# Two gated-mix attention branches on one core: the output product's features put in the order "place by head", one tile of inverted denominators per block, and the output weights rearranged once in DRAM

## The chip, the core and the metric

The kernel runs on one core of a Trainium2 chip. The metric is the time of the slowest core (here the only one) in microseconds of one execution, taken on the device. The work is split among TensorE (PE, with its weight loads PEld), VectorE (DVE), ScalarE (ACT), GpSimd (POOL) and SyncE (SP), whose only work here is to issue every DMA of the kernel.

## What is computed

The same attention layer is computed twice on one input x (2048 tokens, 640 features), with the weights of a branch A and of a branch B, and the two results are mixed by a gate of each token. Each branch has 32 heads of 20 features and treats the tokens in 4 segments of 512:

```
q, k, v = x @ wq, x @ wk, x @ wv               # 32 heads of 20
g = sigmoid(beta)                              # one per head
M, z = 0, 0
for s in range(4):                             # segments of 512 tokens
    logits = qs @ ks.T * 20**-0.5 + mask       # causal within the segment
    a_dot = softmax(logits) @ vs
    a_mem = (phi(qs) @ M) / (phi(qs) @ z + 1e-6)
    o = g * a_mem + (1 - g) * a_dot
    M, z = M + phi(ks).T @ vs, z + sum(phi(ks))
branch = concat(o) @ wo
out = gate * branch_A + (1 - gate) * branch_B  # gate = sigmoid(x . gate_w)
```

Here phi(t) is t + 1 above zero and exp(t) below.

## The kernel before

The work is cut into 8 **blocks** t = 0..7: block t is segment t // 2 of branch t % 2. Within a block there are 8 **quads** of four heads (i = 8 t + u). Products are formed with activations and weights split into a high and a low part (hi, lo), as three terms. TensorE's array is used as two halves of 64 rows that run different instructions side by side (`ROWS`).

Per block, `job_qk` and `job_v` form q, k and v. The parts of q and k are written to DRAM (`hi_lo_out`, L724) and read back by quad with the features of one head on the partitions (`load_quads`, L1136). `s_unit` (L1178) forms the scores and VectorE takes each row's maximum straight out of the PSUM bank (L1165); the maximum is sent into the q tile by a small DMA (L1215). `t_unit` (L1268) forms the transposed scores, ScalarE exponentiates (L1260) and GpSimd clears what lies above the diagonal (L1261). `pv_unit` (L1288) multiplies by v with a column of ones, so row 20 of each head's 32 rows is the softmax denominator; the result is copied to SBUF (L1318). For blocks 0 to 6 `send_dot` writes it to the DRAM tile `dots[t]` (L1332): 32 heads of 32 rows, 512 tokens long. Block 7 goes another way (`fin_unit`), which the change leaves in the order by feature.

For blocks 0 to 6 the softmax numerators then have to be divided by their denominators, weighed with the gates and added to the memory's part. This stage, called the **mix** below, goes as follows. `spread` (L644, L646) lays the token gate out over 16 heads. `reciprocals(t, g, d)` works on half g of the heads: it fetches the 16 denominator rows as a 128 x 64 tile `dn` (L1374), multiplies and inverts them on VectorE (L1354, L1356), writes them to `recs` (L1359), and widens each row 20 times in DRAM into `wide[t]` (L1364, 640 KB read and written). `mix(t, k, y, r)` then fetches, for 128 of the 640 features, the numerators from `dots[t]` in 2 or 3 pieces (L1413: 120, 100, 16, 12, 8 or 4 rows, cut where a head straddles the edge) and the widened inverses from `wide[t]` (L1414), and multiplies the two on VectorE or GpSimd (L1410, L1411). With the memory's part, transposed on TensorE from the tile O (L1493) and added on VectorE (L1473), it is split into hi and lo (L1391 to L1394), and `job_o` multiplies it by the output weights wo (L1018). The first half of the heads can be mixed when the quads 0 to 3 of the block are done, the second when all 8 are.

The order of all instructions is written by a **planner** inside the kernel. It keeps a clock, a list of due times and a queue for each engine, and it emits an instruction when its model says that its inputs have arrived. `dma(us, emit, then, ...)` is what it assumes of a transfer: `us` of bandwidth and `lat` until it has landed. The table `RULES` holds, for each quad, eight numbers that shift its choices. On the chip every engine runs its list in the order written: what the planner believed too early is waited for, with everything behind it on that engine. The tiles `row0` to `row27` (`big`) are a pool of 128 x 512 buffers, shared by all stages. The framework gives SP's transfers eight semaphores in turn, and an issue waits for the transfer eight places before it to have landed.

The lines of `mix` that load:

```
for f, n, src in parts_of:
    dma(0.0055 * n, ... out=r32(y[f:f + n, :]), in_=src ...)          # L1413
dma(0.7, ... out=r32(r), in_=wide[t][P * k:P * k + P, :] ...)          # L1414
```

Of the kernel before, what the change touches and what calls it, by code (L numbers as in the profile page):

```python
# [18 lines left out]
P = 128  # L19
D = 640  # L20
# [22 lines left out]
def tile_gated_mix_infini_attn(  # L43
# [122 lines left out]
    def start_next(e):  # L166
# [11 lines left out]
        def end():  # L178
            busy[e] = False
            load[e] -= dur  # L180
            if then:
                at(clk[0] + DONE[e], then)
# [1584 lines left out]
```

## Time and profile before

| What | Value |
|---|---|
| Times of three runs | 1053.37, 1049.56, 1052.10 us; median 1052.1 us |
| The profiled execution's own time | 1050.84 us |
| Its span, first to last instruction | 1049.1 us |
| Mean granted TensorE clock | 0.989 |
| TensorE busy (weight loads) | 1014.1 us (858.9 us) |
| VectorE, ScalarE, GpSimd busy | 758.6, 661.2, 582.6 us |
| DMA engines' mean share, bytes moved | 77.5%, 249.5 MB |
| Issues of SP | 1133 |

The profile is one execution. A row of its groups reads: line, engine, operation, output<-input by the program's names, sizes, count, then busy time and mean of one instruction, then how long the engine sat idle just before such instructions and what ended that. `bank` is a PSUM bank, `row` a buffer of the pool, `wst` a tile of raw weights, `wh` and `wl` its two parts. A view of stretches gives, for each stretch of the span, the busy time and count of each engine, the granted clock, the DMA engines' mean busy share and the GB/s that they moved. The view of the DMA queue in order of time gives start, time and line of each run of issues on SP; the time is that of issuing, not of landing.

### The profile page before, as it was taken

To read this page: it belongs to the slowest core of one execution; us is meant where nothing else is said; L and a number is where in the kernel's file an instruction comes from. 1 tells how busy PE (TensorE), PEld (TensorE's weight loads), DVE (VectorE), ACT (ScalarE), POOL (GpSimd) and SP (SyncE) were. 2 spreads that over 40 slices of the span, in tenths; PEclk is the share of its full clock that TensorE was granted. 3 is DMA by queue.
4 is the path that set the end of the run, shared out by engine and by line. 5 is a ranking of instruction groups with operands and counts; after the bars stand their busy time and mean duration, and the time that the engine had idled before them with its cause. 6 is when DMAs were issued, how large, how long until landed. Compare 5 with 4: busy or idle time off the path is not lost.

```text
span 1049.1 us, 31149 instructions
## 1 busy us (share of the span) xinstructions
PE 1014.1 (97%) x11260; PEld 858.9 (82%) x11260; DVE 758.6 (72%) x2632; ACT 661.2 (63%) x1344; POOL 582.6 (56%) x1020
## 2 busy tenths in 40 slices
PE   9999998999999999989999999999999999999998
PEld 7888887788887898878889777887888977778876
DVE  4777786766796777866778776788667866776854
ACT  6377676577655566746756556575666665666472
POOL 4455565556454655755655655575565545647271
PEclk9999999999999999989999999999999999998999
DMA  7898978878787888867978778897779878868631
GB/s 258 281 314 242 304 229 260 245 252 260 198 270 216 262 270 247 282 185 236 288 202 268 207 253 264 246 285 206 244 241 272 259 236 259 265 187 258 166 119 55
DMA packets 138399, 251.53 MB, mean 240 GB/s; under 512 B 20085, under 2 KB 24213, under 8 KB 138245
## 3 DMA queue, kind: packets, MB, share of 16 engines
q1 hardware_dynamic: 138244, 249.54, 77.5%
q8 instruction: 89, 1.46, 0.6%
q14 instruction: 66, 0.53, 0.2%
HBM read 159.88 MB, written 97.96 MB: 246 GB/s over the span
## 4 chain that ended last, share of the span: by engine, by line
PE 70%; DMA 16%; DVE 4%; SPq 4%; ACT 2%; issue 2%; POOL 2%; DVEq 0%; ACTq 0%; POOLq 0%
PE bank L744 41%; PE bank L1288 11%; PE bank L1268 6%; PE bank L1178 6%; DMA row<-wide 4%; PE bank L934 2%; PE bank L854 2%; PE bank L894 2%; SPq L1413 2%; DVE bank L1165 2%; DMA wst<-in_b_wv_dram 1%; DMA qd<-row 1%; DMA qst<-qd 1%; DMA row<-dots 1%; DMA kst<-kd 1%
## 5 line engine op out<-in xcount | busy, mean ns | idle before, releaser
L1165 DVE CUSTOM_DVE_ANT_0 bank<-bank,tri 128x384 f32<-128x384 f32 (+3 forms) x1024 | 475.3, 520 | 155.2 <-PE bank L1178 119.1
L744 PE MATMUL bank<-row,wh 64*128 64x512 f32 x2308 | 503.8, 404 | 1.1 <-DVE row L701 1.1
L1260 ACT ACTIVATE p<-bank 128x512 f32<-128x512 f32 x582 | 319.9, 600 | 138.8 <-PE bank L1268 102.7
L1261 POOL TENSOR_SCALAR_AFFINE_SELECT p<-p 128x256 f32<-128x256 f32 (+1 forms) x582 | 217.8, 384 | 251.6 <-ACT p L1260 239.0
L744 PEld LDWEIGHTS bank<-row,wh 64*128 64x128 f32 x2308 | 318.4, 186 | 13.6 <-DVE row L701 1.3
L744 PE MATMUL bank<-row,wl 64*128 64x512 f32 x1154 | 304.7, 401 | 0.0
L536 POOL TENSOR_TENSOR wl<-wst,wh 128x640 fp32r<-128x640 f32 x115 | 180.1, 1570 | 66.2 <-ACT wh L534 64.1
L1268 PE MATMUL bank<-qst,kst 62*128 62x384 f32 (+3 forms) x1024 | 180.9, 323 | 17.8 <-DVE mx L1165 7.0
L1178 PE MATMUL bank<-kst,qst 60*128 60x384 f32 (+3 forms) x1024 | 181.3, 318 | 5.4 <-DVE mx L1165 3.3
L744 PE MATMUL bank<-wvh,row 64*128 64x320 f32 x1280 | 184.8, 316 | 0.7 <-DVE mx L1165 0.7
L744 PEld LDWEIGHTS bank<-row,wl 64*128 64x128 f32 x1154 | 178.3, 187 | 5.5
L1268 PEld LDWEIGHTS bank<-qst,kst 62*128 62x128 f32 x1024 | 132.6, 188 | 30.3 <-DVE mx L1165 10.2
L744 PEld LDWEIGHTS bank<-wvh,row 64*128 64x128 f32 x1280 | 153.3, 187 | 2.6 <-DVE mx L1165 0.9
L1178 PEld LDWEIGHTS bank<-kst,qst 60*128 60x128 f32 x1024 | 133.6, 187 | 15.3 <-DVE mx L1165 5.9
L1288 PE MATMUL bank<-p,vst 128*32 128x256 f32 (+3 forms) x1920 | 145.6, 427 | 0.2 <-DVE mx L1165 0.2
L1165 DVE DVE_READ_ACCUMULATOR2_ANT mx<- 128x1 f32 x1024 | 145.6, 142 | 0.0
L1288 PEld LDWEIGHTS bank<-p,vst 128*32 128x32 f32 x1920 | 58.6, 110 | 85.0 <-issue 62.1
L744 PE MATMUL bank<-wvl,row 64*128 64x320 f32 x640 | 105.3, 313 | 0.0
L534 ACT CAST wh<-wst 128x640 fp32r<-128x640 f32 x119 | 87.0, 742 | 28.1 <-PE bank L744 14.0
L744 PEld LDWEIGHTS bank<-wvl,row 64*128 64x128 f32 x640 | 84.3, 186 | 0.2
L511 POOL TENSOR_TENSOR wvl<-wst,wvh 128x640 fp32r<-128x640 f32 (+1 forms) x48 | 63.9, 1336 | 21.4 <-ACT wvh L508 20.4
L1318 ACT COPY row<-bank 128x512 f32<-128x512 f32 x55 | 32.5, 592 | 56.2 <-PE bank L1288 45.8
(117 smaller groups left out, 1175.7 us busy)
## 6 DMA issues: line engine op xcount, KB each, us to landing
qd<-row SPq DMA_DIRECT2D x120, 256.0 KB
kd<-row SPq DMA_DIRECT2D x120, 256.0 KB
qst<-qd SPq DMA_DIRECT2D x128, 240.0 KB
kst<-kd SPq DMA_DIRECT2D x128, 240.0 KB
dots<-row SPq DMA_DIRECT2D x56, 256.0 KB
wide<-recs SPq DMA_DIRECT2D x14, 640.0 KB
row<-wide SPq DMA_DIRECT2D x35, 256.0 KB
wst<-in_a_wq_dram SPq DMA_DIRECT2D x20, 320.0 KB
```

The costliest lines, as they stand in the source:

```text
L511: put("G", 0.77 * n, lambda: nc.gpsimd.tensor_tensor(out=wl[:, a:b, :], in0=w3, in1=r32(wh[:, a:b, :]), op=ALU.subtract), end, prio=4)
L534: put("A", 0.625, lambda: nc.scalar.copy(wh, w3), lambda: put(lo_eng, lo_cost, lambda: lo.tensor_tensor(out=wl, in0=w3, in1=r32(wh), op=AL ...
L536: lambda: lo.tensor_tensor(out=wl, in0=w3, in1=r32(wh), op=ALU.subtract), end, prio=3), prio=6)
L744: return nc.tensor.matmul(bank_of, lhsT=w[ROWS[half]], rhs=x_[ROWS[half]], start=start, stop=stop)
L854: return nc.tensor.matmul(pm[:, a - h0:c - h0, :].rearrange("p h e -> p (h e)"), lhsT=r32(pqTs[t, m][ROWS[half], P * n:P * (n + 1)]), rhs= ...
L1165: put("D", w / 960.0 + 0.105, lambda: nc.vector.tensor_tensor_reduce(out=sc[:, off:off + w], in0=sc[:, off:off + w], in1=tri[:, L - w:], s ...
L1178: lane_ops[half].append((mm(w), lambda pair=pair, qb=qb, off=off, w=w, r=r, sc=sc: nc.tensor.matmul(sc[:, off:off + w], lhsT=q[r, pair, P ...
L1260: put("A", 0.483, lambda: nc.scalar.activation(pt, sc, AF.Exp, scale=SCALE), lambda: (bank.give(sc), put("G", 0.15 + 0.105 * len(todo), la ...
L1261: "G", 0.15 + 0.105 * len(todo), lambda: nc.gpsimd.affine_select(out=blocks, in_=blocks, pattern=[[0, len(todo)], [1, P]], base=0, channel ...
L1268: lane_ops[half].append((mm(w), lambda pair=pair, kb=kb, off=off, w=w, r=r, sc=sc: nc.tensor.matmul(sc[:, off:off + w], lhsT=k[r, pair, P ...
L1288: nc.tensor.matmul(po[32 * j:32 * j + 32, P * kb:], lhsT=vst[t % 2][:, kb, h * E1:h * E1 + 32], rhs=pts[i, n, f][0][:, off:off + w], start ...
L1318: either(0.483, lambda: nc.scalar.copy(r32(oT), po), 0.605, lambda: nc.vector.tensor_copy(r32(oT), po), end, 2)
```

## The change

1. Features of the output product. The 640 features of blocks 0 to 6 are put in the order "place e within the head, then head h" (32 e + h), where they stood in the order 20 h + e. The memory's part is written to the tile O in that order (`by_head`, at L871), so a tile of 128 features holds 4 places of all 32 heads.
2. Loads of the mix. With that order the numerators of one tile are one DMA, 4 places by 32 heads (L1434 of the new kernel), in place of 2 or 3 pieces.
3. Inverted denominators. The 128 lanes of every one of the five feature tiles need the same 32 inverses, four times over. So one tile d of 128 x 512 is fetched (L1392, the denominators of all heads, 4 times), multiplied with the token gate, fetched straight from `rowg` to all partitions (L1394), and inverted in two halves of 256 columns. It serves all five multiplies. `spread`, `recs`, `wide`, the two halves of heads and their tiles go away; the mix of a block starts when all 8 quads are done.
4. Output weights. wo of both branches must have its rows in the new order. `mix_weights` does it once in DRAM, from due times 75 and 215 of the planner's clock: five DMAs to `wrow` (row-major), five to `wmix` (rows reordered, 4 places by 32 heads each). 35 loads of wo (blocks 0 to 6) then read 5 pieces of 128 columns per partition from `wmix`; the five of block 7 stay as they were.
5. The high part of q and k goes to its two places in DRAM with one DMA of 512 KB in place of two of 256 KB.
6. The planner: SP's next issue also waits until the eighth-last transfer is assumed to have landed; the assumed times of most transfers are raised (0.7 to 0.82 or 0.87, 0.84 to 1.05) and their latencies lowered (2.0 to 1.6); `RULES` is another table. With it the order of the instructions differs throughout the program.

SP issues 940 DMAs in place of 1133, counted in the two programs. TensorE has the same number of matmuls.

```diff
     RULES = {
-        0: "TSTSTSTSTS 1.010 1.98 0.35 8 0.0 1.6 1.92",
...
+        0: "TSTSTSTSTS 1.010 2.38 0.30 8 0.0 1.6 1",
...
-        if e == "S" and dma_free[0] > clk[0] + BACKLOG:
...
+        if e == "S":
+            begin_at = max(dma_free[0] - BACKLOG, lands[-LANES] if len(lands) >= LANES else 0.0)
...
+        if kind == "o":
+            src = [wmix[t % 2].rearrange("k p n -> p k n")[:, :, P * c:P * c + P] for c in range(KT)]
...
+    def mix_weights(b):
+        def rows(k):
+            if k == KT:
+                blocks(0)
+                return
+            dma(2.0, lambda: nc.sync.dma_start(
+                out=wrow[b][k].rearrange("p (m n) -> p m n", n=P),
+                in_=weights[b]["o"].rearrange("m p k n -> k p m n")[k]), prio=500)
+            at(clk[0] + 3.0, lambda: rows(k + 1) if k + 1 < KT else at(clk[0] + 6.0, lambda: blocks(0)))
+
+        def blocks(c):
+            heads = wrow[b].rearrange("k p n -> (k p) n").rearrange("(h e) n -> e h n", e=DH)
+            dma(2.0, lambda: nc.sync.dma_start(
+                out=wmix[b][c].rearrange("(e h) n -> e h n", h=H), in_=heads[4 * c:4 * c + 4]),
+                (lambda: mixed_there.add(b)) if c == KT - 1 else None, prio=500)
...
-                for c in places:
-                    dma(0.7, lambda c=c, part_=part_: nc.sync.dma_start(
-                        out=r32(dst[P * m:P * (m + 1), c, :]), in_=r32(part_)), one, prio=-1)
+                dma(0.7 * n, lambda n=n, places=places, part_=part_: nc.sync.dma_start(
+                    out=r32(dst[P * m:P * (m + 1), places, :]),
+                    in_=r32(part_)[:, None, :].to_broadcast([P, n, L])), sent, prio=-1)
...
+        rec_asked.add(t)
+        big.want((F32, F32), lambda d, g: reciprocals(t, d, g), prio=1)
         for k in range(KT):
...
+            big.want((F32,), lambda y, k=k: mix(t, k, y), prio=2)
+
+    def lanes_of(t):
+        return dots[t].rearrange("(h r) n -> r h n", r=32)
+
+    def reciprocals(t, d, g):
+        def gates():
+            put("D", 0.605, lambda: nc.vector.scalar_tensor_tensor(
+                out=r32(d), in0=r32(d), scalar=gcol[t % 2], in1=r32(g), op0=ALU.mult, op1=ALU.mult), lambda: half(0), prio=2)
+
+        def half(c):
+            cols = slice(L // 2 * c, L // 2 * (c + 1))
+            put("D", 1.78, lambda: nc.vector.reciprocal(r32(d[:, cols]), r32(d[:, cols])),
+                (lambda: half(1)) if c == 0 else done, prio=2)
...
+        dma(0.8, lambda: nc.sync.dma_start(
+            out=r32(d), in_=lanes_of(t)[DH:DH + 1, :, :].to_broadcast([4, H, L])), landed, prio=-1, lat=1.6)
...
-        for f, n, src in parts_of:
-            dma(0.0055 * n, lambda f=f, n=n, src=src: nc.sync.dma_start(out=r32(y[f:f + n, :]), in_=src), landed, prio=0, lat=1.8)
-        dma(0.7, lambda: nc.sync.dma_start(out=r32(r), in_=wide[t][P * k:P * k + P, :]), landed, prio=0, lat=1.8)
+        dma(0.82, lambda: nc.sync.dma_start(out=r32(y), in_=lanes_of(t)[4 * k:4 * k + 4, :, :]), landed, prio=0, lat=1.6)
```

VectorE's list at the mix of block 3, second half of the heads before and the whole block after; `mx` is the row maxima of `s_unit`, `row_11667` and `row_11674` are numerators and the row named beside each its widened inverses. Before:

```order
L871 TENSOR_TENSOR O_178<-bank_157,mw_1_1_9455 128x260
L1165 ISA bank_158,mx_9224<-bank_158,tri 128x512
L1165 ISA mx_9224 128x1
L1165 ISA bank_154,mx_9224<-bank_154,tri 128x512
L1165 ISA mx_9224 128x1
L1410 TENSOR_TENSOR row_11667_9382<-row_11667_9382,row_11668_9383 128x512
L1410 TENSOR_TENSOR row_11674_9384<-row_11674_9384,row_11675_9385 128x512
L1473 TENSOR_TENSOR row_11659_9379<-bank_157,row_11659_9379 128x512
L1165 ISA bank_158,mx_9551<-bank_158,tri 128x512
```

Two multiplies stand between one quad's maxima and the next one's, with the third on GpSimd. After, on the same engine and block (`row_10577` is the tile of inverses, `row_10586`, `row_10592` and `row_10595` three of the five tiles of numerators):

```order
L1375 SCALAR_TENSOR_TENSOR row_10577_8935<-row_10577_8935,gcol_133,row_10578_8936 128x512
L737 TENSOR_TENSOR row_10661_8988<-bank_137,row_10660_8987 128x512
L1380 RECIPROCAL row_10577_8935<-row_10577_8935 128x256
L727 SCALAR_TENSOR_TENSOR row_10662_8989<-bank_137,row_10662_8989 128x512
L737 TENSOR_TENSOR row_10702_9019<-bank_136,row_10701_9018 128x512
L1380 RECIPROCAL row_10577_8935<-row_10577_8935 128x256
L727 SCALAR_TENSOR_TENSOR row_10703_9020<-bank_136,row_10703_9020 128x512
L1425 TENSOR_TENSOR row_10586_8939<-row_10586_8939,row_10577_8935 128x512
L1425 TENSOR_TENSOR row_10592_8941<-row_10592_8941,row_10577_8935 128x512
L1425 TENSOR_TENSOR row_10595_8942<-row_10595_8942,row_10577_8935 128x512
L1192 ISA bank_137,mx_9080<-bank_137,tri 128x512
```

The inversion and three multiplies now stand together, and the next quad's maxima (L1192, L1165 of before) behind the last of them.

SP's list at the same place. Before, the second half's loads, behind the widening in DRAM:

```order
L1364 DMA wide_134<-recs_127 320x1x512
L1332 DMA dots_121<-row_11488_9216 128x512
L1413 DMA row_11659_9379<-dots_120 4x512
L1413 DMA row_11659_9379<-dots_120 120x1x512
L1413 DMA row_11659_9379<-dots_120 4x512
L1414 DMA row_11660_9380<-wide_134 128x512
L1413 DMA row_11667_9382<-dots_120 16x512
L1413 DMA row_11667_9382<-dots_120 100x1x512
L1413 DMA row_11667_9382<-dots_120 12x512
L1414 DMA row_11668_9383<-wide_134 128x512
L1413 DMA row_11674_9384<-dots_120 8x512
L1413 DMA row_11674_9384<-dots_120 120x1x512
```

After, the whole block's loads:

```order
L1392 DMA row_10577_8935<-dots_120 128x1x512
L1394 DMA row_10578_8936<-rowg_125 128x512
L1434 DMA row_10583_8938<-dots_120 128x1x512
L1434 DMA row_10586_8939<-dots_120 128x1x512
L1434 DMA row_10589_8940<-dots_120 128x1x512
L1434 DMA row_10592_8941<-dots_120 128x1x512
L1434 DMA row_10595_8942<-dots_120 128x1x512
L1163 DMA qst_80<-qd_101 60x2x512 x2
L1163 DMA kst_84<-kd_109 60x2x512
L750 DMA qd_101<-row_10660_8987 128x2x512
```

Seven issues in one run, with the next quad's q and k (`qst`, `kst`, L1136 of before) and the writes of q (`qd`) behind them. In blocks 0, 2 and 4 the later four tiles of numerators stand up to 15 rows further down, where the pool had no free buffer.

More of the change, by code (lines that the diff above doesn't have):

```diff
@@ L180, in end @@
             load[e] -= dur
-            if then:
+            if then and e == "S":
+                then()
+            elif then:
                 at(clk[0] + DONE[e], then)
@@ L377, in tile_gated_mix_infini_attn @@
     dots = [dram.tile([32 * H, L], F32, name=f"dots{i}") for i in range(7)]
[L378 to L379 removed]
     rowg = [dram.tile([2 * NB, P], F32, name=f"rowg{s}") for s in range(NSEG)]
[L381 to L383 removed]
+    wrow = [dram.tile([KT, P, D], F32, name=f"wrow{b}") for b in range(2)]
+    wmix = [dram.tile([KT, P, D], F32, name=f"wmix{b}") for b in range(2)]
+    gcol = [const.tile([P, 1], F32, name=f"gcol{b}") for b in range(2)]
     NBIG, NWST, NWH, SPARE = 28, 3, 4, 2
@@ L616, in segment_gate @@
             over_sigmoid(gate[:, s, b, :], pg[:, c], sign)
[L618 to L619 removed]
+    rows_there = set()
     def row_gates(s):
@@ L630, in gone @@
             mr_store.give(gr)
-            for t in range(2 * s, min(2 * s + 2, 7)):
-                row_store.want(1, lambda r, t=t: spread(r, t), prio=t)
+            rows_there.add(s)
+            dots_ready(2 * s)
+            dots_ready(2 * s + 1)
         def got(gr):
@@ L1341, in dots_ready @@
+        rec_asked.add(t)
+        big.want((F32, F32), lambda d, g: reciprocals(t, d, g), prio=1)
         for k in range(KT):
-            if (t, k) not in dot_asked and (t, 6) in dot_there and all(
-                    (t, h // 4) in dot_there and (t, h // 16) in rec_there for h in range(LO[k], HI[k] + 1)):
-                dot_asked.add((t, k))
-                big.want((F32, F32), lambda y, r, k=k: mix(t, k, y, r), prio=2)
-    def reciprocals(t, g, d):
-        rows = slice(16 * g, 16 * g + 16)
-        def landed():
-            put("D", 0.75, work, written, prio=2)
-        def work():
-            nc.vector.scalar_tensor_tensor(
-                out=d, in0=d, scalar=gcol[t % 2][:, g:g + 1], in1=row_gate[t], op0=ALU.mult, op1=ALU.mult)
-            nc.vector.reciprocal(d, d)
-        def written():
-            dma(0.1, lambda: nc.sync.dma_start(
-                out=recs[t][rows, :].rearrange("h (a n) -> (h a) n", n=SPAN), in_=d), widen, prio=-1, some=True, lat=1.4)
-        def widen():
-            dn_store.give(d)
-            dma(1.8, lambda: nc.sync.dma_start(
-                out=wide[t][DH * 16 * g:DH * 16 * (g + 1), :].rearrange("(h e) n -> h e n", e=DH),
-                in_=recs[t][rows, None, :].to_broadcast([16, DH, L])), over, prio=-1, issue=0.69)
-        def over():
-            rec_there.add((t, g))
-            if (t, 1 - g) in rec_there:
-                row_store.give(row_gate.pop(t))
-            dots_ready(t)
-        dma(0.1, lambda: nc.sync.dma_start(
-            out=d, in_=dots[t].rearrange("(h r) (a n) -> h r a n", r=32, n=SPAN)[rows, DH, :, :]), landed, prio=-1, lat=2.0)
@@ L1378, in weighed, with mix @@
+    waiting = {}
+    weighed_of = {}
+    def mix(t, k, y):
         def weighed():
-            big.give(r)
+            weighed_of[t] = weighed_of.get(t, 0) + 1
+            if weighed_of[t] == KT:
+                big.give(inverse.pop(t))
             if t < 2:
```

124 lines of the change are left out of this document (62 added, 62 removed), and 114 rows, old and new, of the table RULES.

## Prediction, made before the changed kernel was run

> **What bounds the kernel now.** I read the page first, then the waits by engine, then stretches of the span around the mix, and last the order of VectorE and SP there.
>
> The page's totals, engine by engine:
>
> ```profile
> span 1049.1 us, 31149 instructions
> PE 1014.1 (97%) x11260; PEld 858.9 (82%) x11260; DVE 758.6 (72%) x2632; ACT 661.2 (63%) x1344; POOL 582.6 (56%) x1020
> DMA packets 138399, 251.53 MB, mean 240 GB/s; under 512 B 20085, under 2 KB 24213, under 8 KB 138245
> q1 hardware_dynamic: 138244, 249.54, 77.5%
> ```
>
> TensorE is the bound: it idles 1049.1 - 1014.1 = 35.0 us in all. The change leaves its matmuls alone, so it can win about those 35 us, plus what TensorE loses where only one half of its array runs, and it can lose much more. Next, nine stretches around the mix of blocks 0 to 6 (busy time of each engine, weight loads after PE, then clock, DMA share, GB/s):
>
> ```profile
> 157.40:209.80 52.40, 46.97 (x513) 37.14 (x509) 36.84 (x121) 32.52 (x66) 30.04 (x52) 1.00 0.87 253
> ...
> 304.00:332.00 28.00, 26.07 (x308) 23.11 (x308) 20.70 (x76) 16.45 (x34) 10.38 (x22) 1.00 0.78 235
> 440.00:466.00 26.00, 22.23 (x243) 19.55 (x240) 16.17 (x62) 11.29 (x24) 14.13 (x27) 0.87 0.75 218
> ...
> 920.00:936.00 16.00, 14.16 (x159) 11.94 (x157) 11.33 (x41) 8.49 (x18) 6.50 (x14) 0.89 0.62 168
> sum 220.40, PE 199.87 PEld 168.12 DVE 158.56 ACT 122.03 POOL 110.40; mean PE 22.21 PEld 18.68 DVE 17.62 ACT 13.56 POOL 12.27
> ```
>
> In these 220.4 us, a fifth of the span, TensorE idles 220.40 - 199.87 = 20.5 us, more than half of its idle time. So the stage that the change rebuilds is where the time is lost. What waits there, in the list of waits (total, times, longest):
>
> ```profile
> DVE row L1410 <- DMA row<-wide: 35.9, 19, 3.6
> ...
> DVE dn L1354 <- DMA dn<-dots: 4.6, 3, 3.1
> ...
> POOL row L1411 <- DMA row<-wide: 7.6, 3, 3.7
> ```
>
> VectorE stands 35.9 us at its multiply for a load, with the maxima that would free TensorE's banks queued behind it. One instance in detail, block 1: SP's issues, VectorE's two multiplies, and TensorE in steps of 2 us.
>
> ```profile
> 308.26 1.73 SPq L1413 DMA_DIRECT2D row<-dots  x3
> ...
> 314.68 1.10 SPq L1413 DMA_DIRECT2D row<-dots  x2
> 315.83 0.46 SPq L1414 DMA_DIRECT2D row<-wide  x1
> ```
>
> ```profile
> 319.58 0.69 DVE L1410 TENSOR_TENSOR row<-row,row 128x512 f32<-128x512 f32 x1 [0.59 <-DMA row<-wide]
> 323.45 0.69 DVE L1410 TENSOR_TENSOR row<-row,row 128x512 f32<-128x512 f32 x1 [3.18 <-DMA row<-wide]
> ```
>
> ```profile
> 322.00:324.00 2.00, 1.10 (x10) 0.57 (x8) 0.55 (x1) 0.00 (x0) 0.00 (x0) 1.00 1.07 249
> 324.00:326.00 2.00, 1.00 (x9) 0.83 (x11) 2.00 (x7) 1.82 (x5) 0.31 (x2) 1.00 1.04 280
> ```
>
> The last load was issued at 315.83 and VectorE went on at 323.45. Of VectorE's 3.18 us wait TensorE idled 4.00 - 2.10 = 1.9 us, so about 1.3 us of such a wait is covered by banks still full.
>
> **Why those loads are late.** The list of issues (sizes per issue):
>
> ```profile
> qst<-qd SPq DMA_DIRECT2D x128, 240.0 KB
> ...
> row<-wide SPq DMA_DIRECT2D x35, 256.0 KB
> ...
> row<-dots SPq DMA_DIRECT2D x21, 240.0 KB
> row<-dots SPq DMA_DIRECT2D x14, 200.0 KB
> qst<-mr SPq DMA_DIRECT2D x128, 8.0 KB
> ...
> rowg<-mr SPq DMA_DIRECT2D x4, 4.0 KB
> beta<-in_a_beta_dram SPq DMA_DIRECT2D x1, 16.0 KB
> ```
>
> The 37 rows of that list add to 1133 issues. The page counts 20,085 packets under 512 B. Data explain 4736 of them (35 issues of dn, recs and rg with 128 pieces of 256 B, two of beta with 128 of 128 B). I read the other 15,349 as marks of completion, one from each DMA engine that took part. Sixteen per issue would be 18,128. The 2780 that lack are what comes out, but for one, if a copy runs on as many engines as divide both sides' outer index: q and k loads (outer 60) on 15, `qst<-mr` on 2, `rowg` on 8, and the numerators' pieces on 6, 5, 12, 8, 4 and 4 by their heads or rows. So a 240 KB piece puts 20 rows of 2 KB on each of six engines, where `row<-wide` puts 8 on each of sixteen; what follows waits for the full ones.
>
> [...] Were every copy spread over sixteen, term B below would be zero and my sum about 1037; by the rule it is 1070.
>
> **The change, part by part.** Durations, by line and shape:
>
> ```profile
> L1410 DVE TENSOR_TENSOR row<-row,row 128x512 f32<-128x512 f32 x26 | 19.0, 730 | 37.0 <-DMA row<-wide 35.9 <-DMA kst<-kd 1.1
> L1411 POOL TENSOR_TENSOR row<-row,row 128x512 f32<-128x512 f32 x9 | 11.5, 1282 | 9.3 <-DMA row<-wide 7.6 <-DMA row<-dots 1.6
> L1354 DVE SCALAR_TENSOR_TENSOR dn<-dn,gcol,rg 128x64 f32<-128x64 f32 x14 | 10.0, 715 | 4.6 <-DMA dn<-dots 4.6
> L1356 DVE RECIPROCAL dn<-dn 128x64 f32<-128x64 f32 x14 | 7.7, 553 | 0.5
> L870 DVE RECIPROCAL mw<-mw 128x19 f32<-128x19 f32 x24 | 6.6, 276 | 0.8
> L701 DVE SCALAR_TENSOR_TENSOR row<-bank,row 128x512 f32<-128x512 f32 x29 | 19.7, 685 | 1.2 <-ACT row L705 1.2
> ```
>
> A. *The old path goes* (`spread`, dn, recs, wide, the cut numerators). With it goes the wait above: at most the 20.5 us of idle time in the mix stretches, at least nothing if a new wait stands in its place. I take all 20.5 off here and price the new wait in B.
>
> B. *The new loads of the mix.* `d` and the five `y` are 4 places by 32 heads: outer index 4, so four engines carry 32 rows of each, 6 x 32 = 192 rows a block, in one run of issues. Before, the second half put 20 + 20 + 20 = 60 on its fullest engines, and VectorE waited 3.18 us. In proportion the last numerators are 3.18 x 192 / 60 = 10.2 us late. Some of that is hidden: the multiplies need the inverse anyway. It costs one multiply (685 ns) and two reciprocals; from 276 ns at 19 columns and 553 at 64, a column is 6.16 ns, so 256 columns are 1.74 us, and 0.69 + 2 x 1.74 = 4.2 us. That leaves 6.0 us of wait, 4.7 after the 1.3 that banks cover, times seven blocks: **+33**. Queued behind the waiting multiply on VectorE are the next quad's maxima, for them TensorE's banks; behind the loads on SP, the next quad's q and k, also on the full engines. Bounds: 0 (as fast as `row<-wide`) to 7 x (10.2 - 1.3) = 62. I stand nearer the middle because blocks 0, 2 and 4 issue their loads in pieces.
>
> C. *Output weights in DRAM.* Ten issues with 640 packets to `wrow`, outer index 128, harmless; ten of 320 KB to `wmix`, outer index 4: 160 rows of 2.5 KB in each of two batches, as many bytes on four engines as a mix. No engine waits for them directly; what passes them on the same engines is late. Bounds 0 to 2 x 10.2 = 20; I take **+6**, since they are issued apart. The 35 weight loads in 512 B pieces instead of 2560 B ones move the same bytes; they lie a few places ahead of use (cover: `wst` has three tiles). If that cover fails, ScalarE's split waits; nearest row, the wait of 3.6 us at the mix, so 0 to 7; I take 0.
>
> D. *VectorE.* Seven times 0.69 + 3.48 = 29.1 us replace 10.0 + 7.7 = 17.7: +11.4 us on an engine that is busy 72%. What counts is that a reciprocal holds the maxima 1.74 us instead of 0.55; 14 x 1.2 = 17 at most, 0 at least; **+3**. GpSimd gets 13 more multiplies and subtractions (50 for 37), 13 x 1.28 = 17 us; it is idle 44% of the span, and if that cover fails, the clearing of p is late, which I leave in the range.
>
> E. *Fewer issues.* 1133 - 940 = 193 less, 80 of them by writing the high parts twice in one DMA. Removed bytes: wide 14 x 640 KB and 35 x 256 KB; added: 14 x 256 KB, 20 x 320 KB; some 9 MB of 249.5 net. TensorE's idle time outside the mix is 35.0 - 20.5 = 14.5 us, the start and end included, so 0 to -10; **-4**.
>
> F. *The new table and assumed times* move every instruction. Nothing in the trace prices that; I put plus or minus 8 into the range and 0 into the sum. The write into O with steps of 32 elements has the same count of elements; 0.
>
> Sum: -20.5 + 33 + 6 + 3 - 4 = +17.5 on the profiled execution's 1050.8; its span is 1.7 shorter than its time, and the median of three runs 1.3 above it. On the median: 1052.1 + 17.5, about **1070 us**.
>
> **The rivals.**
>
> 1. *The loads hide, and it is faster.* If the numerators land while the inverse is computed, B is nearly nothing: 1052.1 - 20.5 + 3 - 4 = 1031, or 1037 with C. For it: everything from denominator to product is a third as many DMAs, and the planner now counts transfers in flight. Against: it assumes 0.82 us for each `y`, as for a load over all engines. It decides where the last `y` lands within 4.2 + 1.3 = 5.5 us of when it was due. Chance 0.31.
>
> 2. *The waits trade places.* VectorE's wait at the new multiply equals the old one's 35.9 us; TensorE idles as before; within 5 us of 1052. Chance 0.11.
>
> 3. *Four engines become the bound.* q and k loads, too, stand behind the bursts (in 574 to 578 us of the trace before, below, the mean share falls to 0.62 while narrow pieces are outstanding). With B and C at their upper ends: 1052.1 - 20.5 + 62 + 20 + 3 - 4 = 1113. Chance 0.08.
>
> ```profile
> 570.00:574.00 4.00, 4.00 (x63) 4.00 (x62) 3.27 (x12) 2.77 (x7) 1.63 (x4) 1.00 0.85 273
> 574.00:578.00 4.00, 4.00 (x59) 3.97 (x57) 3.54 (x18) 1.09 (x2) 0.86 (x3) 1.00 0.62 162
> ```
>
> **How the numbers follow.** My forecast, slower by narrow loads (1058 to 1098, the upper end being B at its 62 with C at 6: 1052.1 - 20.5 + 62 + 6 + 3 - 4), 0.50; rival 3, 0.08; no change, 0.11; faster, 0.31. A measurement of this kernel tells about 0.5%, 5 us, from no change, so faster 0.31, same 0.11, slower 0.58. Both signs are likely: the range reaches down to 1028 (rival 1 without C, less a third of the table's 8) and up to 1098, which leaves out the fastest part of rival 1 and rival 3.
>
> **What would show it.** Right: in the profile after, VectorE (L1425) and GpSimd wait for `row<-dots` longer than the 43.5 us of before, in single waits of 5 us and more, TensorE idles just after, and the mean DMA share falls then. Wrong: those waits together under 20 us (B), or TensorE's idle time at some place that has no mix (C, F). If the `y` loads land as fast as `row<-part` or `xT` loads do, the reading of the marks is wrong.

## The result, and the profile after

The changed kernel takes 1114.5 us (median of three runs, 1113.5 to 1116.5) against 1052.1 before: a ratio of 1.060, 95% interval 1.056 to 1.064. It is slower, as forecast, but by 62 us where 18 were forecast, and it lies above the range of 1028 to 1098. The number is the one that rival 3 gave, 1113, at a chance of 0.08.

The page of the kernel after, the same rows as were shown of before, and its mean granted clock:

```profile
span 1114.7 us, 30803 instructions
PE 1040.0 (93%) x11260; PEld 884.7 (79%) x11260; DVE 772.2 (69%) x2605; ACT 661.7 (59%) x1347; POOL 595.4 (53%) x1033
DMA packets 149223, 241.99 MB, mean 217 GB/s; under 512 B 12592, under 2 KB 45520, under 8 KB 149072
q1 hardware_dynamic: 149072, 240.03, 70.3%
```

```profile
core 0: 1114.7 us, clock 0.959
```

TensorE idles 1114.7 - 1040.0 = 74.7 us, 39.7 more than before. That is not all: the same 11,260 matmuls are also busy 25.9 us longer. Together 65.6 us, the whole difference of the two spans. Fewer bytes pass (240.0 MB for 249.5), yet the DMA engines' share falls from 77.5% to 70.3% and the rate from 240 to 217 GB/s: the time does not go to more bytes.

The seven stretches around the mix of blocks 0 to 6, in that order (length, busy time of TensorE, weight loads, VectorE, ScalarE, GpSimd; then clock, DMA share, GB/s):

```profile
183.00:215.00 32.00, 22.59 (x184) 18.72 (x185) 18.80 (x51) 16.43 (x33) 16.62 (x27) 0.79 0.59 185
313.00:338.00 25.00, 17.64 (x169) 13.24 (x166) 15.16 (x33) 9.29 (x19) 9.08 (x15) 0.80 0.64 204
455.00:490.00 35.00, 26.16 (x283) 23.45 (x285) 22.39 (x58) 14.42 (x30) 14.67 (x20) 0.76 0.53 160
596.00:612.00 16.00, 9.26 (x93) 8.70 (x92) 10.21 (x13) 5.64 (x12) 4.86 (x8) 0.87 0.67 214
735.00:770.00 35.00, 23.58 (x263) 21.04 (x265) 23.61 (x60) 15.86 (x33) 14.22 (x19) 0.83 0.58 171
875.00:900.00 25.00, 16.23 (x176) 15.53 (x175) 14.10 (x22) 8.59 (x17) 8.14 (x13) 0.69 0.71 214
1003.00:1023.00 20.00, 12.21 (x119) 10.99 (x121) 12.51 (x32) 4.89 (x11) 6.18 (x8) 0.86 0.66 213
sum 188.00, PE 127.68 PEld 111.67 DVE 116.77 ACT 75.11 POOL 73.77; mean PE 18.24 PEld 15.95 DVE 16.68 ACT 10.73 POOL 10.54
```

TensorE idles 188.0 - 127.7 = 60.3 us in them, against 20.5 in the mix stretches of before. Outside them it idles 74.7 - 60.3 = 14.4 us, against 14.5. So the whole new idle time is at the mix; there the clock is granted at 0.69 to 0.87, and the DMA engines stand at 53% to 71%.

What waits for a DMA, the longest of the list (total, times, longest):

```profile
POOL row L1426 <- DMA row<-dots: 37.0, 9, 8.8
DVE row L1425 <- DMA row<-dots: 34.1, 10, 6.8
DVE row L1375 <- DMA row<-rowg: 20.2, 5, 6.6
ACT wh L539 <- DMA wst<-wmix: 19.5, 4, 13.4
ACT row L584 <- DMA row<-in_xT_dram: 17.7, 6, 8.3
ACT wh L539 <- DMA wst<-in_a_wk_dram: 16.6, 5, 6.5
```

and the last two of the kernel before, for comparison:

```profile
ACT row L554 <- DMA row<-in_xT_dram: 7.6, 8, 3.1
...
ACT wh L534 <- DMA wst<-in_a_wk_dram: 4.0, 4, 2.3
```

VectorE and GpSimd wait 34.1 + 37.0 = 71.1 us for the numerators (L1425, L1426), 43.5 before. But as much again, 74.0 us, stands below: VectorE for the gate row, ScalarE for output weights, xT and k weights. These four copies are wide ones: each has 16 completion marks in the trace, where a load of numerators has four. What makes them late is shown by the marks below.

One instance, block 5. SP's issues, VectorE, and TensorE in steps of 3.41 us (busy times, then clock, DMA share, GB/s):

```profile
867.82 6.46 SPq L1434 DMA_DIRECT2D row<-dots  x4
874.38 4.08 SPq L750 DMA_DIRECT2D kd<-row  x2
...
886.51 0.59 SPq L1434 DMA_DIRECT2D row<-dots  x1
```

```profile
894.92 0.69 DVE L1425 TENSOR_TENSOR row<-row,row 128x512 f32<-128x512 f32 x1 [6.77 <-DMA row<-dots]
```

```profile
870.00:874.00 4.00, 4.00 (x64) 2.89 (x58) 2.52 (x6) 2.71 (x7) 2.62 (x3) 1.00 0.30 95
874.00:877.56 3.56, 1.78 (x24) 1.44 (x22) 2.20 (x5) 2.22 (x5) 1.17 (x4) 1.00 0.28 106
...
884.38:887.79 3.41, 1.47 (x28) 1.33 (x25) 1.25 (x4) 0.75 (x2) 1.04 (x3) 1.00 0.28 108
887.79:891.20 3.41, 3.00 (x38) 3.00 (x39) 0.35 (x1) 0.00 (x0) 0.00 (x0) 0.50 0.74 197
891.20:894.60 3.40, 0.42 (x2) 0.20 (x1) 0.00 (x0) 0.00 (x0) 0.00 (x0) 0.50 0.95 236
894.60:898.00 3.40, 1.73 (x16) 1.74 (x18) 3.08 (x5) 1.75 (x3) 1.05 (x1) 0.50 0.94 225
898.00:901.44 3.44, 3.44 (x24) 3.44 (x24) 2.88 (x6) 1.27 (x3) 3.44 (x4) 0.50 1.01 239
901.44:904.80 3.36, 3.36 (x40) 3.33 (x39) 3.07 (x12) 0.00 (x0) 0.95 (x1) 1.00 1.00 202
```

Four loads of numerators take SP 6.46 us, where one alone takes 0.59: SP itself is held up, and the writes of k and q stand behind. The longest of SP's own waits from 864 to 898:

```profile
SPq L1434 <- DMA row<-dots: 3.2, 1, 3.2
```

From 870 to 877.6 the mean DMA share is 0.30 and 0.28, 4.5 to 4.8 of 16 engines, with some six loads outstanding. The trace's records of the completion marks, grouped by issue (my own grouping: time of issue, copy, number of marks, and how long after the issue the middle one and the last one came), show the rest:

```
867.82  row<-dots L1434   4 marks   middle  9.9   last  9.9 us
877.29  kd<-row   L750   16 marks   middle  2.9   last 11.0 us
878.55  qd<-row   L750   16 marks   middle  2.9   last 11.0 us
887.72  kst<-kd   L1163  15 marks   middle  3.5   last  8.2 us
```

In each of the two writes (16 marks) twelve marks have come after 2.9 us, and four need 8.5 to 11.0. Of the 15 marks of the k load eleven have come after 3.9 us, and four need 5.9 to 8.2. Each time four marks are late, as many as a load of numerators has; I read them as the four engines that the narrow loads fill. The last load of numerators is issued at 886.5 and VectorE goes on at 894.9. TensorE idles in that wait, and for 13.65 us, from 887.79 to 901.44, it is granted half its clock: 24 matmuls in 3.44 us, where the next step has 40 in 3.36.

### The profile page after: what moved, and what is told of

It is laid out like the page before. It is cut to its first block, busy times and chain, and to the rows that moved or that the text cites. A ratio compares the mean times of both kernels' runs of the same rounds, so it can differ in the third digit from the quotient of the medians.

```text
span 1114.7 us, 30803 instructions
## 1 busy us (share of the span) xinstructions
PE 1040.0 (93%) x11260; PEld 884.7 (79%) x11260; DVE 772.2 (69%) x2605; ACT 661.7 (59%) x1347; POOL 595.4 (53%) x1033
## 2 busy tenths in 40 slices
DMA packets 149223, 241.99 MB, mean 217 GB/s; under 512 B 12592, under 2 KB 45520, under 8 KB 149072
## 3 DMA queue, kind: packets, MB, share of 16 engines
q1 hardware_dynamic: 149072, 240.03, 70.3%
## 4 chain that ended last, share of the span: by engine, by line
PE 73%; DMA 18%; issue 3%; DVE 3%; POOL 1%; ACT 1%; SPq 1%; POOLq 0%; DVEq 0%; ACTq 0%
PE bank L771 42%; PE bank L1315 11%; DMA row<-dots 7%; PE bank L1205 6%; PE bank L1295 6%; DMA row<-in_xT_dram 3%; PE bank L961 3%; DMA wst<-wmix 2%; PE bank L881 2%; PE bank L921 2%; DMA qd<-row 1%; DVE bank L1192 1%; PE bank L1230 1%; DMA kst<-kd 1%; DMA wst<-in_b_wv_dram 1%
## 5 line engine op out<-in xcount | busy, mean ns | idle before, releaser
L1192 DVE CUSTOM_DVE_ANT_0 bank<-bank,tri 128x128 f32<-128x128 f32 (+3 forms) x1024 | 475.1, 521 | 166.9 <-PE bank L1205 130.4
L1287 ACT ACTIVATE p<-bank 128x512 f32<-128x512 f32 x574 | 314.8, 600 | 149.9 <-PE bank L1295 125.9
L1288 POOL TENSOR_SCALAR_AFFINE_SELECT p<-p 128x256 f32<-128x256 f32 (+1 forms) x574 | 211.6, 377 | 262.4 <-ACT p L1287 243.9
L771 PEld LDWEIGHTS bank<-row,wh 64*128 64x128 f32 x2308 | 322.2, 187 | 11.1 <-DVE O L898 0.6
L771 PE MATMUL bank<-wvh,row 64*128 64x320 f32 x1280 | 199.1, 329 | 8.9 <-DVE row L1493 4.6
L1205 PE MATMUL bank<-kst,qst 60*128 60x128 f32 (+3 forms) x1024 | 185.4, 322 | 19.2 <-DVE row L737 7.0
L1295 PE MATMUL bank<-qst,kst 62*128 62x128 f32 (+3 forms) x1024 | 181.4, 323 | 12.3 <-DVE mx L1192 9.6
L771 PEld LDWEIGHTS bank<-wvh,row 64*128 64x128 f32 x1280 | 161.7, 196 | 12.5 <-DVE row L1493 4.9
L1205 PEld LDWEIGHTS bank<-kst,qst 60*128 60x128 f32 x1024 | 138.3, 190 | 29.4 <-DVE row L737 7.3
L1315 PE MATMUL bank<-p,vst 128*32 128x512 f32 (+3 forms) x1904 | 146.5, 431 | 0.5 <-POOL p L1288 0.4
L1192 DVE DVE_READ_ACCUMULATOR2_ANT mx<- 128x1 f32 x1024 | 144.4, 141 | 0.0
L539 ACT CAST wh<-wst 128x640 fp32r<-128x640 f32 x119 | 87.0, 739 | 57.5 <-DMA wst<-wmix 19.5
L771 PE MATMUL bank<-wvl,row 64*128 64x320 f32 x640 | 110.0, 322 | 0.0
L1345 ACT COPY row<-bank 128x512 f32<-128x512 f32 x60 | 35.3, 589 | 68.9 <-PE bank L1315 63.9
```

The source lines that it names most:

```text
L539: put("A", 0.625, lambda: nc.scalar.copy(wh, w3), lambda: put(lo_eng, lo_cost, lambda: lo.tensor_tensor(out=wl, in0=w3, in1=r32(wh), op=AL ...
L771: return nc.tensor.matmul(bank_of, lhsT=w[ROWS[half]], rhs=x_[ROWS[half]], start=start, stop=stop)
L1192: put("D", w / 960.0 + 0.105, lambda: nc.vector.tensor_tensor_reduce(out=sc[:, off:off + w], in0=sc[:, off:off + w], in1=tri[:, L - w:], s ...
L1205: lane_ops[half].append((mm(w), lambda pair=pair, qb=qb, off=off, w=w, r=r, sc=sc: nc.tensor.matmul(sc[:, off:off + w], lhsT=q[r, pair, P ...
L1287: put("A", 0.483, lambda: nc.scalar.activation(pt, sc, AF.Exp, scale=SCALE), lambda: (bank.give(sc), put("G", 0.15 + 0.105 * len(todo), la ...
L1288: "G", 0.15 + 0.105 * len(todo), lambda: nc.gpsimd.affine_select(out=blocks, in_=blocks, pattern=[[0, len(todo)], [1, P]], base=0, channel ...
```

## The experiments

The theory after this reading: outer index 4 puts each load of the mix on four DMA engines, and what costs time is that everything issued behind it queues for these four, not only that VectorE waits in order for its own operands. The rivals: that only VectorE's and GpSimd's own waits count; that the rows lie 64 KB apart in DRAM; that the table, the rearranged output weights or the run of issues on SP do it. All ratios are to the kernel before, run on the same chip as the experiment.

| Kernel | ratio, 95% interval | TensorE idle, busy (us) | clock |
|---|---|---|---|
| before | 1 | 35.0, 1014.1 | 0.989 |
| after | 1.060 (1.056 to 1.064) | 74.7, 1040.0 | 0.959 |
| e1_wide | 0.986 (0.982 to 0.991) | 18.1, 1008.0 | 0.997 |
| e9_wide_again | 0.981 (0.978 to 0.984) | 18.5, 1008.0 | 0.997 |
| e2_wide_wmix4 | 0.987 (0.984 to 0.991) | 20.6, 1008.4 | 0.997 |
| e5_split4 | 1.005 (1.002 to 1.008) | 33.1, 1023.1 | 0.983 |
| e6_split2 | 1.161 (1.154 to 1.168) | 163.3, 1049.1 | 0.921 |
| e10_idle_wide | 1.003 (1.000 to 1.006) | 35.3, 1017.2 | 0.987 |
| e11_idle_narrow | 1.069 (1.065 to 1.072) | 94.4, 1026.2 | 0.958 |
| e4_told | 1.076 (1.072 to 1.080) | 60.2, 1065.9 | 0.958 |
| e3_table_before | 1.116 (1.113 to 1.120) | 77.9, 1083.8 | 0.955 |
| e7_wide_table_before | 1.047 (1.041 to 1.053) | 32.7, 1064.1 | 0.976 |
| e8_before_table_after | 1.071 (1.065 to 1.076) | 51.4, 1068.3 | 0.976 |
| e12_one_half | 0.974 (0.971 to 0.978) | 14.1, 1002.9 | 0.999 |

**Wide loads.** The features are put in the order 4 h + e within a tile, so the loads walk the heads first.

```diff
-        return dots[t].rearrange("(h r) n -> r h n", r=32)
+        return dots[t].rearrange("(h r) n -> h r n", r=32)
...
-        dma(0.82, ... in_=lanes_of(t)[4 * k:4 * k + 4, :, :]) ...
+        dma(0.82, ... in_=lanes_of(t)[:, 4 * k:4 * k + 4, :]) ...
...
-                out=wmix[b][c].rearrange("(e h) n -> e h n", h=H), in_=heads[4 * c:4 * c + 4]),
+                out=wmix[b][c].rearrange("(h e) n -> h e n", h=H), in_=heads[:, 4 * c:4 * c + 4, :]),
```

The memory's part is written into O in that order too (last section); the order of the instructions stays.

> The changed kernel in the same order of instructions, with one thing undone: within a tile of 128 features the order is head first, then place (4 h + e), so the loads of the numerators, of the denominators and the copies into wmix have 32 as their outer index and not 4. Theory N (copies with outer index 4 run on four DMA engines, and what waits for them or behind them is late): the sum without the term for the new loads, about 1037 us, and 1015 to 1045 in any case; the waits of VectorE and GpSimd for row<-dots fall from 71 us to under 20. Theory T (the new table and the new order of instructions are what is slow): the order is the same, so within 10 us of 1114. Theory V (the inversion of a whole tile on VectorE, 1.7 us at a time, holds up the maxima): within 15 us of 1114.

Measured: 0.986, and 0.981 when run again (e9). VectorE and GpSimd sit idle only 1.6 and 1.7 us before their multiplies (rows in the last section). The seven stretches of the same lengths, set by the two reciprocals of each block (the first and the sum):

```profile
177.76:209.76 32.00, 31.34 (x312) 25.23 (x308) 27.64 (x81) 22.79 (x46) 24.80 (x38) 1.00 0.87 258
...
sum 188.00, PE 179.17 PEld 159.13 DVE 172.05 ACT 113.08 POOL 132.51; mean PE 25.60 PEld 22.73 DVE 24.58 ACT 16.15 POOL 18.93
```

TensorE idles 188.0 - 179.2 = 8.8 us in them, against 60.3 after and 20.5 before. With 32 as the outer index of the loads the change is faster than before by 1.4 to 1.9%, and this is the fastest complete version of those tried. It says that the order of the features decides; not yet whether by the number of engines, by the distance of the rows, or by the write into O.

**The rearranged weights alone narrow** (e1_wide with only the copies to `wmix` walking the places first):

> The kernel of e1, but the ten copies into wmix again with outer index 4. Theory N: they cost what term C said, 6 us (0 to 20) above e1. If only the loads of the mix matter: the same as e1 within 3 us.

Measured: 0.987 beside 0.986, 1.3 us on 1052 (2.7 us in the medians), inside both intervals, which are 3 to 5 us wide on each side. Nothing is to be seen of C's narrow copies; a cost of a few microseconds would not be.

**Same rows, same order, only the pieces.** Each load of d and y as four DMAs of one place by 32 heads (outer index 32), or as two of two places (outer index 2); no instruction of another engine moves.

```diff
-        dma(0.82, lambda: nc.sync.dma_start(out=r32(y), in_=lanes_of(t)[4 * k:4 * k + 4, :, :]), ...
+        dma(0.82, lambda: [nc.sync.dma_start(
+            out=r32(y)[32 * e:32 * (e + 1)],
+            in_=lanes_of(t)[4 * k + e:4 * k + e + 1, :, :]) for e in range(4)], ...
```

> The kernel after, every instruction of every engine in the same order, except that each of the 42 mix loads (d and five y, 4 places by 32 heads) is issued as four DMAs of one place by 32 heads in a row: the same rows of the same DRAM tiles to the same partitions, outer index 32 in place of 4. Theory (outer index 4 puts a load on four DMA engines, and everything else queues behind these four): most of the 7.5% between after and e1_wide comes back, less what 126 more issues cost on SP (24 issues in a run, about 0.5 us each, so the last y is 10 us late once more but holds no engine): ratio to before 0.99 to 1.03. Rival 1 (the rows lie 64 KB apart in DRAM, and that is what is slow; e1_wide read four neighbouring rows): no gain, ratio 1.05 to 1.07. Rival 2 (what costs is that one run of loads holds SP and the eight transfers in flight): more issues make it worse, ratio above 1.07.

> As e5_split4, but two DMAs of two places by 32 heads each: outer index 2. Theory: both go to the same two DMA engines, which then carry 192 rows each per pair and 384 a block where four carried 192 each; the last y lands twice as late as after (some 20 us late), so the loss against e1_wide at least doubles: ratio to before 1.13 to 1.25. Rival 1 (distance of the rows in DRAM): as after, 1.05 to 1.07. Rival 2 (number of issues in a run): between after and e5_split4.

Measured: 1.005 and 1.161. Four pieces bring back 5.5 of the 7.4 points between after and e1_wide, two pieces cost 10 points more. Neither the distance of the rows nor the number of issues does that: both kernels read the same rows, and the one with more issues is the faster. The pieces' marks in the page of e5_split4 also count as expected:

```profile
DMA packets 151745, 242.02 MB, mean 229 GB/s; under 512 B 15112, under 2 KB 48040, under 8 KB 151592
```

Forty-two loads with 4 x 16 marks in place of 4 are 42 x 60 = 2520 more, and 12,592 + 2520 = 15,112. Two engines for four made the loss against e5_split4 2.8 times as large (15.6 points for 5.5). Both halves of a load went to the same two engines: in the trace of e6_split2 the k load issued at 968.98 us has 13 of its 15 marks within 4.1 us, and the two others after 11.1 and 11.6.

**Is it the waiting for one's own load, or the queue for everybody?** In e4_told the planner is told landings of the kernel after's kind (11 us for `y`, 6 us for d and the gate row, in place of 1.6), so that it puts their users later.

> The changed kernel, whose planner is told that the numerators land 11 us after their turn in place of 1.6, and d and the gate row 6 us; the loads themselves are as narrow as before. If the harm is that engines stand in order at a load that the planner believed there: VectorE and GpSimd wait under 25 us for row<-dots, and the time falls to 1060 to 1080. If the harm is that four DMA engines hold up every other copy too: it stays above 1095, with the waits moved to other loads.

Measured: 1.076, slower than after. The waits of the kernel e4_told for DMAs, in the same columns as above:

```profile
ACT wh L539 <- DMA wst<-wmix: 17.7, 5, 10.3
...
ACT row L584 <- DMA row<-in_xT_dram: 15.2, 6, 11.9
...
DVE row L1425 <- DMA row<-dots: 14.2, 5, 5.4
...
PE bank L1205 <- DMA kst<-kd: 12.4, 3, 11.4
...
POOL row L1426 <- DMA row<-dots: 4.1, 3, 3.0
```

VectorE's and GpSimd's waits for numerators fall from 71.1 to 18.3 us and the time does not come back: TensorE itself now waits for k (11.4 us at once), ScalarE for xT 11.9 at once. That the own waits alone cost the time is unlikely. But the order of the planner moves here too, and TensorE is busy 25.9 us longer than after, so this run alone does not decide it.

The next two take the own waits away altogether. They are e1_wide with six more copies of 256 KB behind the last load of each mix, from `dots` to tiles that nobody reads, once with outer index 32, once with 4.

```diff
+    def idle_copies(t, k):
+        for j in range(6 if k == KT - 1 else 0):
+            nc.sync.dma_start(
+                out=idle_copy[t][j].rearrange("(e h) n -> e h n", h=H),
+                in_=dots[t].rearrange("(h r) n -> r h n", r=32)[j:24:6])
```

> The kernel of e1_wide once more, on the chip of the three runs below, which are all built from it: ratio to before 0.98 to 0.99.

> e1_wide, every instruction in the same order, and behind the last load of each of the seven mixes six more copies of 256 KB from dots to DRAM tiles that nobody reads, outer index 32 (16 engines); no result depends on them. Both theories: 2 x 11 MB more on the DMA engines and 42 issues: 0 to 1.5% above e9_wide_again.

> The same rows copied as in e10_idle_wide, with outer index 4, so on four engines, again for nobody. Theory (a narrow burst costs by what it does to everybody else's copies: gate rows, xT, weights, q and k): at least half of the 7.5% between after and e1_wide, so 3.5 to 7% above e10_idle_wide, with waits of ScalarE and GpSimd for wst, row<-in_xT and q or k that e10 does not have. Rival (what cost time was VectorE and GpSimd standing in order at their own late numerators): within 1% of e10_idle_wide, since the mix's own loads were issued before.

Measured: 0.981, 1.003, 1.069. The wide copies cost 2.3%, more than was expected of them; the narrow ones 1.069 / 1.003, 6.6% more, for the same bytes and as many issues. The waits of e11_idle_narrow:

```profile
ACT wh L541 <- DMA wst<-wmix: 32.9, 5, 17.4
ACT row L586 <- DMA row<-in_xT_dram: 30.2, 5, 14.8
POOL row L590 <- DMA row<-in_xT_dram: 15.2, 1, 15.2
ACT wh L541 <- DMA wst<-in_b_wq_dram: 12.7, 1, 12.7
```

No engine stands for its load at a multiply of the mix here. Copies that no instruction waits for make the kernel slower by nearly as much as the mix's own narrow loads do (6.6% and some 7.5%). The marks behind one such burst: the k load issued at 886.06 us has eleven of its 15 marks within 3.7 us and four after 9.6 to 9.9, and VectorE's next maxima begin at 896.21, after 9.70 us without work. SP is held up as well, but little more than by the wide copies: its own waits for landings add to 67.7 us here and to 55.5 in e10_idle_wide, while the medians differ by 65.5 us. So the queue of the four full engines is the mechanism, and it needs no waiting operand of its own.

**The table.** The tables were exchanged: that of before in the kernel after (e3), that of before in e1_wide (e7), that of after in the kernel before (e8).

> The changed kernel with the table RULES of before; all else as changed. Theory N: the narrow loads are still there, so still 1095 to 1125. Theory T: back towards the kernel before, under 1075.

> e1_wide with the table RULES of the kernel before. Theory (the table was worth 5% in e3_table_before only because it sets where late loads are waited for): with loads in time it is worth little, ratio to before 0.98 to 1.00, at most 1.5% above e1_wide. Rival (the new table fits the new program in general, whatever the loads do): about 5% above e1_wide, ratio 1.03 to 1.04.

> The kernel before with nothing changed but the table RULES, taken from the kernel after. If the new table is better by itself, and e1_wide owes its gain to it: ratio 0.98 to 0.99. If a table fits the program it was made for and the gain of e1_wide comes from the new mix: ratio 1.00 to 1.04.

Measured: 1.116, 1.047 and 1.071; the first and the last lie outside everything that was expected of them. The exchanged table costs 1.116 / 1.060, 5.3%, in the kernel after; 1.047 / 0.986, 6.2%, in e1_wide; 7.1% in the kernel before. My theory for e7, that a table matters only where loads are late, fell: with loads in time it costs as much. In e7 the loss shows less as idle time (32.7 us for 18.1) than as busy time of TensorE:

```profile
PE 1064.1 (97%) x11260; PEld 893.6 (81%) x11260; DVE 785.0 (72%) x2618; ACT 659.4 (60%) x1339; POOL 599.8 (55%) x1028
```

56 us more than e1_wide's 1008.0 for the same matmuls, with a clock of 0.976 in place of 0.997. Of its busy time 43.3 us lie in stretches at half clock, in e1_wide 6.8; if half of the difference is the loss, the clock makes some 18 of the 56 us (an estimate). The rest was not taken apart; that the two halves of the array run side by side less often is a guess. Neither table is the better one in general: each is better in its own program, and e8 shows that the new table alone does not give the gain of e1_wide.

**The inverses.** e1_wide without the second reciprocal of each block:

> e1_wide without the second of the two reciprocals of each block (columns 256 to 511 of the denominators are not inverted), else in the same order: 7 x 1.74 = 12.2 us less work on VectorE, about what term D of the prediction priced. By that term: 3 us, so 0.3% below e9_wide_again. If every microsecond that a reciprocal holds the row maxima is paid: 12 us, 1.2% below. If VectorE has slack at the mix: the same within 0.3%.

Measured: 0.974 beside e9's 0.981, 6.6 us in the medians, for 12.2 us less on VectorE; the intervals just fail to meet. Between the two expectations: by these runs about half of what a reciprocal holds is paid.

## Why the prediction was wrong in size, step by step

**What bounds, A and E.** That the time is lost at the mix was right: the idle time outside is 14.4 us for 14.5. Without narrow loads the sum gave 1031, or 1037 with C (ratios of 0.980 and 0.986); e1_wide is that kernel, and has 0.986 and 0.981. That the sum of A, D and E fits is in part luck: between the spans of before and e1_wide, 23.0 us, the idle time at the mix gives 11.7 where A took 20.5, the idle time outside it 5.2 where E took 4, and TensorE's busy time 6.1, for which there was no term. E is not to be seen in the kernel after.

**B is the step that failed**: "That leaves 6.0 us of wait, 4.7 after the 1.3 that banks cover, times seven blocks: +33". Narrow loads cost (1.060 - 0.986) x 1052 = 78 us, 83 by the second measurement of e1_wide, with the write into O in both; e5_split4 wins back 58 of it, and between e10 and e11, where the write and the number of issues are the same, narrow copies cost 65.5. B and C had 39. The reading of the marks was right, and the wait that B prices came out near: 7 x 6.0 = 42 us at VectorE's multiply were forecast, 34.1 came. That is partly luck, since the 60 rows in B's proportion leave out the 8 rows of each of three `row<-wide` on the same engines, 24 more. That the narrow copies meet on the same engines, which B takes for granted, the trace after shows: the four loads issued from 867.82 to 871.38 have their last marks one behind the other, at 877.7, 880.3, 882.9 and 886.5, and just four marks of each write behind them are late. What failed is to take this one wait for the whole price. The prediction names the q and k loads behind the burst on the full engines, and then gives them no term; the gate row, xT and GpSimd's own waits (37.0 us) have none either. Per span, from the two traces: mix idle +39.8 us where A to D had -20.5 + 33 + 6 + 3 = +21.5; outside -0.1 where E had -4; and TensorE's busy time +25.9, where I had nothing. 39.8 - 0.1 + 25.9 = 65.6.

**The clock had no term.** The traces of before and after grant two clocks only, 1.00 and 0.50. All stretches at half clock, summed, in the kernel before and then after (their length, then the busy time of each engine in them):

```profile
sum 24.15, PE 18.59 PEld 17.65 DVE 11.22 ACT 10.50 POOL 12.68; mean PE 3.72 PEld 3.53 DVE 2.24 ACT 2.10 POOL 2.54
```

```profile
sum 92.44, PE 67.57 PEld 60.08 DVE 57.06 ACT 39.34 POOL 43.52; mean PE 4.22 PEld 3.76 DVE 3.57 ACT 2.46 POOL 2.72
```

TensorE works 67.6 - 18.6 = 49.0 us more at half clock. If half of that is the loss, it is 24.5 us. In the steps of 3.41 us in which TensorE was busy throughout, it got through 0.55 as much at half clock as at full (14 such steps and 253, in the trace after, each matmul weighed by its kind's mean time at full clock); with that figure the loss is 22 us. Both are estimates, and most of the 25.9. The waits that halved the clock here were thus paid a second time, after they ended.

**"I stand nearer the middle because blocks 0, 2 and 4 issue their loads in pieces"** was no reason: TensorE idles 9.4, 8.8 and 11.4 us in their stretches, and 7.4, 6.7, 8.8 and 7.8 in those of blocks 1, 3, 5 and 6.

**C** was priced at 6 us with both its parts; that its copies are narrow costs 1.3 by e2_wide_wmix4, not to be told from nothing. The cover of the loads from `wmix`, put at 0 with 7 us as its bound, failed behind the narrow loads: ScalarE waits 19.5 us for them after, 3.8 in e1_wide. What the rearrangement costs as a whole wasn't tried. **D**: 3 us for 11.4 us more on VectorE; half of 12.2 us was paid in e12, so it should have been about 6. The reciprocal's own 1.74 us was right (1742 ns in e1_wide).

**F** was put at 0 with a range of 8 us. The 0 stands only since each program has its own table; the exchange of tables is worth 5 to 7%, 55 us and more, in any of the three programs. The sentence "The write into O with steps of 32 elements has the same count of elements; 0" was wrong on VectorE, below.

**Rivals.** Rival 3, "Four engines become the bound", is what happened, with its number; it had B and C at their upper ends, so it came to 1113 by another working than the one that the traces show, and that the number fits is luck. It deserved more than 0.08, since its condition, that others queue behind the bursts, had its row (DMA share 0.62) in the prediction itself. Rival 1 is what the same change does with wide loads. The signs named beforehand came: 71.1 us for `row<-dots` over 43.5, single waits of 5 us and more, TensorE idle just after, no new idle time of TensorE at places without a mix. The DMA share falls too, to 0.28, but in the steps ahead of the wait at VectorE's multiply in block 5; during that wait it is 0.74 to 0.95.

## What to carry to other kernels

Before merging DMAs into one, look at the outermost index of both sides: one issue over 4 engines was 5.5% slower here than four issues over 16 with the same rows, and reordering the features so that the loads walk 32 heads first made the loss a gain. Price a narrow copy by all that is issued behind it, and not by the instruction that waits for it: copies that nobody waited for cost 6.6% more over 4 engines than over 16. And where TensorE's waits grow, add the time that it then loses at half clock: here some 22 to 24.5 us (the estimates above) beside 39.7 us of new idle time.

## What the runs showed of the hardware that was not expected

**Half clock after idle time.** Every stretch at one granted clock in the traces of before and after lasts a whole number of steps of 3.413 us, one to four of them at half clock; only the last stretch, which the program's end cuts, does not. In the stretch of block 5 the granted clock goes to 0.50 at 887.79, after a step in which TensorE was busy 1.47 of 3.41 us, stays there for four steps of 3.41 us, and is back at 1.00 only after the step in which TensorE was busy throughout (3.44 of 3.44 us). With the whole trace after laid out in steps of 3.41 us, 15 of its 16 halvings follow a step in which TensorE was busy 0 to 59% (the other one 94%), and the least busy step that the full clock outlasted was busy 49%.

**Writing with a step of 32 elements.** VectorE's multiply into O, in the kernel after, and then in e1_wide (runs of 4 neighbouring elements):

```profile
L898 DVE TENSOR_TENSOR O<-bank,mw 128x380 f32<-128x380 f32 x24 | 19.4, 809 | 0.8
L898 DVE TENSOR_TENSOR O<-bank,mw 128x260 f32<-128x260 f32 x24 | 14.1, 588 | 0.8
```

```profile
L905 DVE TENSOR_TENSOR O<-bank,mw 128x380 f32<-128x380 f32 x20 | 11.1, 554 | 0.7
L905 DVE TENSOR_TENSOR O<-bank,mw 128x260 f32<-128x260 f32 x20 | 8.6, 429 | 0.7
```

The 24 of each row after include four of block 7, written without steps in 554 and 428 ns. So the means with steps are (24 x 809 - 4 x 554) / 20 = 860 and 620 ns, with runs of four 554 and 429; over the 48 instructions 24 x 0.255 + 24 x 0.159 = 9.9 us of VectorE. The 9.9 us of VectorE can be part of what e5_split4 still lacks to e1_wide; that was not tried apart.

**Multiplies of both engines.** In e1_wide the mix's multiplies take 1217 ns on VectorE and 1464 on GpSimd, where before they took 730 and 1282 alone at their loads:

```profile
L1434 POOL TENSOR_TENSOR row<-row,row 128x512 f32<-128x512 f32 x18 | 26.3, 1464 | 1.7 <-DVE row L1388 1.3 <-DMA dots<-row 0.2
...
L1433 DVE TENSOR_TENSOR row<-row,row 128x512 f32<-128x512 f32 x17 | 20.1, 1217 | 1.6 <-DMA dots<-row 1.5
```

With the loads in time both engines start them together. The single instructions show that they slow each other: the one multiply of VectorE in e1_wide during which GpSimd did nothing took 681 ns, one wholly beside a multiply of GpSimd 1775; of GpSimd's 18, seven took 1707 to 1804 ns and eleven 1267 to 1303.
